# Moving the second batch's first input transfer and its first two transform groups behind the first batch's last transform, in a fused spectral filter and SiLU network

## The chip, the cores and the metric

The kernel runs on one core of one Trainium2 chip. The metric is device time in microseconds (us) of one execution, lower is better. TensorE is called PE below, VectorE DVE, ScalarE ACT, GpSimd POOL and SyncE SP; "SPq" or "ACTq" is such an engine's queue when it issues a DMA transfer.

## The reference, cut to what matters

```python
batch, seq, dim = (8, 3008, 256)
X = np.fft.rfft(x, axis=1)
F = (filt_r + 1j * filt_i)[None, :, :]
y = np.fft.irfft(X * F, n=x.shape[1], axis=1)      # per batch and channel
h = y.reshape(8 * 3008, 256) @ w_in                # w_in: 256 x 2048
g = h * (1.0 / (1.0 + np.exp(-h)))
out = g @ w_out                                    # w_out: 2048 x 256
```

So each of 8 batches is filtered along its sequence of 3008 points, and all 24064 resulting rows go through a two-layer network.

## The kernel before, in words

**The transform.** 3008 is split as 47 x 64 (in fact 94 x 32), and each batch's filter is three stages of small matmuls with tables of cosines and sines. Stage 1 (`stage1`, L339; for the first batch `stage1_first`, L295) takes rows of the input to 94 residues. `forward` (L456), `multiply`, `add` and `inverse` apply the filter. `stage3` (L574) makes the rows of `y`, which the network reads. Between the stages the data changes its layout by a trip through HBM: it is written to a scratch tensor `d1` (after stage 1) or `d2` (after `inverse`) and read back in another order.

**The network.** It is done in 384 steps of 14 matmuls on 128 x 128 tiles (`hidden` and `project`, L743 and L802). In the steady state the next batch's transform is put between these matmuls by a plan of due times (`plan`, L623).

**The ramp.** The first batch has no earlier batch to hide behind. Its whole transform, and the bit-by-bit conversion of the first nine pairs of weight blocks from 64-bit floats (`weights`, `bits`, `converted`, `rounded`, `placed`), run first, in an order written out by hand from L1038 to L1178. The program order of these lines is the order on each engine's queue. What matters for the change:

- `load_two` (L326) loads the second batch's rows for its transform groups 0 and 1: one transfer on SP of 96 rows of 8 KB (768 KB) into `x_all`. Before, it stands at L1113, behind the last `stage1_first`, which read `x_all` for the first batch, and ahead of `weights(8)` (L1114).
- `inverse_first` (L516) and `rows_first` (L531) end the filter for one of six groups `g`. Each group makes two tiles `q` of 256 KB, copied out of PSUM and written to `d2` (L543). ACT copies and issues both tiles of groups 0 to 3 and the first of groups 4 and 5; DVE copies the second tile of groups 4 and 5, and SP issues it. The tiles of group 4 reuse the buffers of group 0, so their copies wait until those transfers have landed.
- `load_t4_rows` (L567) reads the rows back: six transfers of 256 KB on SP (16 rows of 16 KB each), two for each of three parts `k`. Part 2 needs the rows of groups 4 and 5.
- `second["stage1"](u, False)` (L1159) is stage 1 of the second batch for `u` = 0 and 1: two matmuls of 96 x 512 each on PE (L345, four rows of the trace for each `u`) and four copies of the results on ACT (L361). `store_rows` (L369) writes them to `d1` from POOL, four transfers for each `u`; they stand behind a small POOL copy (L1167) that holds POOL until weight block 8 is placed.
- `idle_wide(16)` (L1170) issues 16 matmuls of 96 x 256 whose result nobody reads.
- Four `stage3` groups (L1171) follow, then the reload of the table `wi_t` (L1173), which must wait for them, `load_x(2)` (L1174), which overwrites the buffer that `stage1(0)` reads, and the transfers of later weight blocks.
- Then the network starts with `hidden(0)`, in which L764, L771 and L777 are copies of partial sums on ACT, and L727 combinations on DVE.

Two things are handed out in program order. `bank` (L251) gives each matmul group one of eight PSUM banks in turn, counted by `early[0]`. And in the trace all transfers that SP and ACT issue take eight landing semaphores in turn, in program order; the issue of a transfer waits until the one eight before it has landed.

Of the kernel before, what the change touches and what calls it, by code (L numbers as in the profile page):

```python
# [170 lines left out]
def kernel(  # L171
# [75 lines left out]
    early = [0]  # L247
# [3 lines left out]
    def bank(b, name, spare=None):  # L251


        if early[0] is None and spare in ("x", "yz"):
            return xps.tile([128, 2, C], FP32, name=name, tag=spare)
        if early[0] is None and spare is not None:
            return accps.tile([128, 2, C], FP32, name=name, tag=f"a{spare}")
        if early[0] is None:
            return fps.tile([128, 2, C], FP32, name=name, tag="f")
        early[0] += 1  # L260
        k = early[0] % 8
        if k < 2:
            return fps.tile([128, 2, C], FP32, name=name, tag="f")
        if k > 5:
            return xps.tile([128, 2, C], FP32, name=name, tag="x" if k == 6 else "yz")
        return accps.tile([128, 2, C], FP32, name=name, tag=f"a{k - 2}")
# [688 lines left out]
    def convert_weights(*js):  # L955
        for j in js:
            _, _, e, m, ef, mf, *_ = raws[j]
            nc.scalar.activation(out=ef, in_=e, func=AFT.Relu, bias=bias_t[:, 0:1])
            nc.scalar.activation(out=mf, in_=m, func=AFT.Identity, scale=2.0 ** -20, bias=1.0)
        for j in js:  # L960
            if j in (0, 2, 6, 7, 8):

                e, ef = raws[j][2], raws[j][4]
                nc.scalar.activation(out=ef, in_=ef, func=AFT.Relu, scale=-1.0, bias=bias_t[:, 1:2])
                nc.scalar.activation(out=e, in_=ef, func=AFT.Identity, scale=-float(1 << 23),
                                     bias=bias_t[:, 2:3])
# [42 lines left out]
    def weights(*js, queue=None):  # L1009
        for j in js:  # L1010
            if wide:
                load_weights(j, queue)
# [5 lines left out]
    def converted(*js):  # L1018
        if wide:
            convert_weights(*js)  # L1020
# [9 lines left out]
    def placed(*js, eng=None):  # L1030
        if wide:
            place_weights(*js, eng=eng)
        else:
            for j in js:
                load_exact(j)
# [15 lines left out]
    def idle_wide(n, ps=None, rhs=None):  # L1051

        ps = ps or bank(0, "idle")
        for _ in range(n):
            nc.tensor.matmul(out=ps[:, 0], lhsT=wx_t, rhs=wide_rows if rhs is None else rhs,
                             start=True, stop=True)
# [4 lines left out]
    part, second = spectral(0), spectral(1)  # L1061
# [47 lines left out]
    for k in range(16):  # L1109
        part["stage1_first"](k, 2)  # L1110
        if k in whole:
            part["stage1_first"](whole[k], 3)
    second["load_two"]()  # L1113
    weights(8)  # L1114
    part["forward"](0, fill=4)
    placed(0, 1)
# [34 lines left out]
    for k in range(2):  # L1151
        part["load_t4_rows"](k)
    part["load_t4_rows"](2)
    converted(4, 5)
    placed(2, 3)
    weights(9)
    converted(6, 7)
    for u in range(2):
        second["stage1"](u, False)  # L1159
    converted(8)  # L1160
    rounded(4, 5)
    placed(4, 5)
# [2 lines left out]
    rounded(8)  # L1165
    placed(8)
    gp.tensor_copy(out=gate, in_=w_t[:, 4, A11, 0, 0:1])  # L1167
    for u in range(2):
        second["store_rows"](u)
    idle_wide(16)  # L1170
    for g in range(4):  # L1171
        part["stage3"](g)
    nc.sync.dma_start(out=wi_t, in_=wi_dram.ap())  # L1173
    second["load_x"](2)  # L1174
    weights(10, 11, 12)
# [91 lines left out]
```

## Time and profile before

| | |
|---|---|
| median of 3 runs | 2577.19 us (2576.88 to 2578.64) |
| the profiled execution | 2579.25 us |
| its span in the trace | 2577.4 us |
| PE busy in the span | 2553.1 us, 99% |
| DVE, ACT, POOL busy | 65%, 42%, 17% |
| mean granted PE clock | 0.995 |
| first matmul of `hidden(0)` | 76.94 us |
| DMA in the first 130 us, mean | 223 GB/s |

The views are: the page (busy shares, slices of the span, the chain of work that ended last), the timeline of one engine (start, duration, engine, line, operation, tile written and read, count, and in brackets the idle time before it and what ended it), the windows (busy time by engine, granted PE clock, DMA share and GB/s in a stretch of time), and the chain in order of time (start, duration, what). Rows of the trace for one float32 matmul come in twos: "x32" of `idle` are 16 matmuls.

### The profile page before, as it was taken

Reading aid. Unit: us, or ns where it says so; the run is one execution under the profiler, and the core shown is the slowest. Engines: PE = TensorE matmul, PEld = TensorE weight load, DVE = VectorE, ACT = ScalarE, POOL = GpSimd, SP = SyncE. Lnnn points to the kernel's source line nnn. Section 1 sums busy time; section 2 is a strip of 40 time slices with the busy share of each in tenths; the row PEclk is TensorE's granted clock in tenths of the full one; section 3 lists DMA queues with packets and bytes.
Section 4 is the critical chain, followed back from the end, with each engine's and each line's share of the span. In section 5 each row is a group of like instructions: output and inputs, shape, how many; then the busy total and the mean of one; then the engine's idle time right before and its main releaser. Section 6 shows DMA issues by size and latency. Waiting matters only on the chain.

```text
span 2577.4 us, 47850 instructions
## 1 busy us (share of the span) xinstructions
PE 2553.1 (99%) x18714; PEld 2196.6 (85%) x18714; DVE 1664.4 (65%) x3589; ACT 1090.4 (42%) x3019; POOL 430.3 (17%) x688
## 2 busy tenths in 40 slices
PE   8999999999999999999999999999999999999998
PEld 6688888888888888888888888888888888888987
DVE  7766666676666666666666676666666666555554
ACT  3544444444444444444444444444444444444443
POOL 4212111111122111311121111211121112101101
PEclk9899999999999999999999999999999999999999
DMA  9522232222223222322233122331232211200011
GB/s 291 158 60 52 70 79 63 60 68 72 59 64 69 70 65 55 79 71 67 59 70 80 49 66 59 79 80 46 66 86 64 68 41 34 59 18 16 9 17 16
DMA packets 198554, 171.06 MB, mean 66 GB/s; under 512 B 122068, under 2 KB 173380, under 8 KB 197348
## 3 DMA queue, kind: packets, MB, share of 16 engines
q1 hardware_dynamic: 176056, 117.06, 19.9%
q0 software_dynamic: 17344, 45.70, 5.6%
q10 hardware_dynamic: 4928, 5.24, 0.7%
q8 instruction: 147, 2.41, 0.4%
q14 instruction: 79, 0.65, 0.1%
HBM read 96.07 MB, written 81.26 MB: 69 GB/s over the span
## 4 chain that ended last, share of the span: by engine, by line
PE 96%; DMA 2%; DVE 0%; ACT 0%; issue 0%; SPq 0%; ACTq 0%; DVEq 0%
PE acc L819 44%; PE px L756 26%; PE pyz L756 19%; PE pd L586 3%; PE pb L467 2%; PE pc L510 2%; PE pf L434 1%; DMA filt<-in_filt_i_dram 0%; PE pa L354 0%; DMA w_t<-in_x_dram 0%; DMA d_t<-d_tbl 0%; PE pa L345 0%; DMA x_all<-in_x_dram 0%; DMA d<-q 0%; DMA w_t<-d 0%; DMA t<-d 0%
## 5 line engine op out<-in xcount | busy, mean ns | idle before, releaser
L819 PE MATMUL acc<-g,w_t 128*128 128x256 f32 (+1 forms) x5376 | 1509.2, 375 | 0.4 <-DVE g L727 0.4
L819 PEld LDWEIGHTS acc<-g,w_t 128*128 128x128 f32 x5376 | 1021.6, 190 | 115.7 <-DVE g L727 0.8
L727 DVE TENSOR_TENSOR g<-pyz,abc 128x256 f32<-128x256 f32 (+1 forms) x1152 | 480.0, 417 | 621.6 <-ACT abc L777 356.2
L727 DVE TENSOR_TENSOR g<-g 128x256 f32<-128x256 f32 (+3 forms) x1152 | 599.4, 520 | 196.7 <-ACT g L760 183.5
L756 PE MATMUL px<-ty,w_t 128*128 128x256 f32 (+1 forms) x2304 | 679.4, 377 | 1.1 <-ACT abc L771 0.6
L760 ACT ACTIVATE g<-g 128x256 f32<-128x256 f32 (+1 forms) x1152 | 472.9, 410 | 250.2 <-DVE g L727 250.2
L727 POOL TENSOR_TENSOR s<-s 128x256 f32<-128x256 f32 (+1 forms) x329 | 255.0, 792 | 1417.5 <-DVE s L839 1321.0
L756 PEld LDWEIGHTS px<-ty,w_t 128*128 128x128 f32 x2304 | 432.7, 190 | 65.5 <-issue 6.2
L756 PE MATMUL pyz<-y,w_t 128*128 128x256 f32 (+1 forms) x1536 | 454.0, 377 | 0.0
L756 PEld LDWEIGHTS pyz<-y,w_t 128*128 128x128 f32 x1536 | 283.9, 190 | 47.6 <-DVE g L727 6.8
L771 ACT COPY abc<-px 128x256 f32<-128x256 f32 (+1 forms) x384 | 141.3, 368 | 372.9 <-PE px L756 372.9
L777 ACT COPY abc<-px 128x256 f32<-128x256 f32 (+1 forms) x384 | 141.5, 369 | 339.0 <-PE px L756 338.1
L760 ACT ACTIVATE g<-px 128x256 f32<-128x256 f32 (+1 forms) x384 | 145.8, 380 | 300.9 <-PE px L756 300.8
L756 PE MATMUL px<-y,w_t 128*128 128x256 f32 (+1 forms) x768 | 232.7, 385 | 0.8 <-DVE y L600 0.8
L756 PE MATMUL pyz<-ty,w_t 128*128 128x256 f32 (+1 forms) x768 | 225.8, 376 | 0.3 <-DVE g L727 0.2
L756 PEld LDWEIGHTS px<-y,w_t 128*128 128x128 f32 x768 | 140.4, 190 | 33.0 <-DVE y L606 5.3
L756 PEld LDWEIGHTS pyz<-ty,w_t 128*128 128x128 f32 x768 | 144.5, 190 | 19.2 <-DVE g L727 1.5
L764 ACT COPY abc<-px 128x256 f32<-128x256 f32 (+1 forms) x384 | 135.4, 353 | 52.7 <-PE px L756 52.7
L586 PEld LDWEIGHTS pd<-wi_t,t 48*64 48x64 f32 x3840 | 61.1, 135 | 25.1 <-ACT g L760 16.4
L446 POOL DMA_DIRECT2D d<-tf x144 | 71.6, 504 | 29.2 <-DVE tf L442 29.2
L839 ACT COPY s<-acc 128x512 f32<-128x512 f32 (+1 forms) x94 | 54.2, 577 | 47.6 <-PE acc L819 47.4
L869 DVE STREAM_TRANSPOSE o<-s 128x256 f32<-128x256 f32 x192 | 73.9, 423 | 0.4 <-issue 0.3
(136 smaller groups left out, 1269.9 us busy)
## 6 DMA issues: line engine op xcount, KB each, us to landing
t<-d SPq DMA_DIRECT2D x120, 192.0 KB
t<-d SPq DMA_DIRECT2D x84, 256.0 KB
d<-q POOLq DMA_DIRECT2D x84, 256.0 KB, 2.7
out_dram<-o SPq DMA_DIRECT2D x636, 32.0 KB
d<-tf POOLq DMA_DIRECT2D x144, 96.0 KB, 3.2
xr<-in_x_dram SPq DMA_DIRECT2D x6, 1472.0 KB
x_all<-in_x_dram SPq DMA_DIRECT2D x72, 96.0 KB
x_all<-xr SPq DMA_DIRECT2D x72, 96.0 KB
```

The costliest lines, as they stand in the source:

```text
L446: nc.gpsimd.dma_start(out=d1[k // 2, :, k % 2, n0:n0 + 4], in_=us["tf"][32 * k:32 * k + NS].rearrange("p q n c -> p (q n) c"))
L467: nc.tensor.matmul(out=ps[k][32 * j:32 * j + 32, ri, :], lhsT=d_t[rows, 4 * g + at, ri, :], rhs=rhs, start=True, stop=True)
L586: nc.tensor.matmul(out=ps[h][c0:c0 + 64, cb, i, :], lhsT=t4[rows, i, 128 * cb + c0:128 * cb + c0 + 64], rhs=wi_t[rows, :], start=True, sto ...
L727: eng.tensor_tensor(out=out, in0=in0, in1=in1, op=op)
L756: nc.tensor.matmul(out=out, lhsT=w_t[:, jp, c, 0], rhs=rhs, start=start, stop=True, skip_group_check=True)
L760: nc.scalar.activation(out=g[:, k, 0:n], in_=g[:, k, 0:n] if src is None else src, func=AFT.Silu)
L764: nc.scalar.copy(out=sums[:, 0, 0:n], in_=xo)
L771: nc.scalar.copy(out=sums[:, 1, 0:n], in_=xo)
L777: nc.scalar.copy(out=sums[:, 2, 0:n], in_=xo)
L819: nc.tensor.matmul(out=acc[pair][i][:, h, 0:n], lhsT=w_t[:, jp, c, 1], rhs=g[:, k, 0:n], start=(jp == 0 and h == 0), stop=last, skip_group ...
L839: copy(out=s[:, 2 * i:2 * i + 2, 0:n], in_=acc[pair][i][:, :, 0:n])
L869: v.transpose(out=o[:, :, h, :], in_=results[pair][:, ((2, 6), (4, 1))[chunk][h], :])
```

## The change

`load_two` moves on SP from ahead of `weights(8)` to behind the six read-back transfers. The two `stage1` groups of the second batch move from ahead of `converted(8)` to behind the four `stage3` groups of the first batch. `idle_wide` goes from 16 to 20 and now follows the last `inverse` on PE directly. The bank counter is advanced by 7, so that the groups behind it get other banks.

```diff
             part["stage1_first"](whole[k], 3)
-    second["load_two"]()
     weights(8)
     part["forward"](0, fill=4)
 ...
     part["load_t4_rows"](2)
+    second["load_two"]()
     converted(4, 5)
     placed(2, 3)
     weights(9)
     converted(6, 7)
-    for u in range(2):
-        second["stage1"](u, False)
     converted(8)
 ...
     gp.tensor_copy(out=gate, in_=w_t[:, 4, A11, 0, 0:1])
+    idle_wide(20)
+    early[0] += 7
+    for g in range(4):
+        part["stage3"](g)
+    for u in range(2):
+        second["stage1"](u, False)
     for u in range(2):
         second["store_rows"](u)
-    idle_wide(16)
-    for g in range(4):
-        part["stage3"](g)
     nc.sync.dma_start(out=wi_t, in_=wi_dram.ap())
     second["load_x"](2)
```

## The prediction

> **What bounds the kernel now.** I read the page first: the slices of the granted clock and the chain that ended last.
>
> ```profile
> PEclk9899999999999999999999999999999999999999
> PE 96%; DMA 2%; DVE 0%; ACT 0%; issue 0%; SPq 0%; ACTq 0%; DVEq 0%
> ```
>
> Over 96% of the span PE is the bound. Behind the ramp (to about 87 us) steps of 14 matmuls follow without a gap, at 0.43 us a matmul, and the change takes no matmul out of them. So it is worth what it moves the point where that steady run begins, and nothing else. As that point I take the end of the second matmul of step 1, 86.63 us in the timeline of PE.
>
> Next I read the chain in order of time, for the ramp (start, duration, what).
>
> ```profile
> 43.29 8.54 DMA x_all<-in_x_dram
> ...
> 51.91 0.37 ACTq L543
> ...
> 53.95 3.01 DMA d<-q
> 56.96 0.67 DVE q L541
> ...
> 57.66 4.00 DMA d<-q
> ...
> 62.27 6.70 DMA w_t<-d
> ...
> 69.10 7.12 PE pd L586 x254
> ```
>
> From 43 to 69 us the ramp waits for transfers, and the first of them is `load_two`, which has nothing to do with the first batch. It delays the writes of `d2` twice: they wait behind it in the DMA engines, and the sixth write (51.91) takes its landing semaphore. The trace's landing records give its price. Weight transfers of 256 KB ahead of it land 0.67 us apart (43.69, 44.34, 45.01, 45.71); from 45.71 to 53.69 four more of them and `load_two` land, so `load_two` took 7.98 - 4 x 0.67 = 5.3 us (at least 3.5, the distance from the landing ahead of it, 48.30 to 51.83). Then twelve writes land 0.66 us apart from 54.11 to 61.66: a full queue. The six reads land from 63.20 to 68.97.
>
> Then the timeline of PE:
>
> ```profile
> 53.48 3.70 PE L345 MATMUL pa<-x_all,wx_t 96*128 96x512 f32 x8
> 57.01 7.07 PE L1055 MATMUL idle<-d_t,wx_t 96*128 96x256 f32 x32
> 67.84 0.42 PE L586 MATMUL pd<-wi_t,w_t 48*64 48x47 f32 x2 [3.76 <-DMA w_t<-d]
> 69.10 7.07 PE L586 MATMUL pd<-wi_t,w_t 48*64 48x47 f32 x254 [0.84 <-DMA w_t<-d]
> 76.94 1.19 PE L756 MATMUL px<-y,w_t 128*128 128x256 f32 x2 [0.77 <-DVE y L600]
> ```
>
> The two `stage1` groups (53.48) cost nothing today: PE would wait until 69.1 anyway. Last, windows that I cut at the clock's own steps. It rises at 8.05, falls at 66.07 and rises at 86.55 us, which are 17 and 6 times 3.413 us apart (columns: stretch, then busy us of PE, PE loads, DVE, ACT, POOL; granted clock, DMA share, GB/s).
>
> ```profile
> 62.66:66.07 3.41, 1.42 (x7) 0.92 (x5) 3.34 (x8) 3.38 (x7) 0.00 (x0) 1.00 0.97 231
> 66.07:69.49 3.42, 0.81 (x18) 0.70 (x19) 3.38 (x9) 2.23 (x4) 0.00 (x0) 0.50 0.83 186
> 69.49:72.90 3.41, 3.41 (x140) 3.41 (x136) 2.00 (x5) 0.95 (x3) 0.88 (x3) 0.50 0.03 8
> 72.90:76.31 3.41, 3.28 (x122) 3.11 (x117) 0.61 (x2) 1.31 (x4) 3.37 (x7) 0.50 0.61 156
> 76.31:79.73 3.42, 2.79 (x7) 1.86 (x7) 2.66 (x6) 0.74 (x2) 0.00 (x0) 0.50 0.82 217
> 83.14:86.55 3.41, 3.41 (x8) 2.63 (x9) 2.02 (x6) 1.46 (x4) 0.00 (x0) 0.50 1.08 290
> 11.46:14.87 3.41, 2.37 (x16) 2.18 (x16) 2.64 (x7) 3.38 (x6) 0.00 (x0) 1.00 1.02 432
> ```
>
> A window with PE busy 1.42 of 3.41 us loses the clock, one with 2.37 keeps it. At half clock two windows full of `stage3`'s small matmuls do not bring it back, nor does one with 2.79 us; a full one of large matmuls does (83.14).
>
> **The change, part by part.**
>
> *Landing of the rows.* Without `load_two` ahead, weight 8 lands 5.3 us earlier, the first write at about 48.8 (50.6 by the lower price), and the writes no longer queue: they come as ACT makes them, one each 1.03 us (copies at 44.72, 45.74, 46.77). The tenth on ACT is issued at 45.32 + 9 x 1.03 = 54.6 instead of 56.11. DVE's copy at 54.88 had waited 3.70 us for the buffer of a write that landed at 54.76; now it follows group 4's matmuls at about 51.8 (four `inverse` groups fill 46.38 to 53.48, 1.77 each), then 0.6, four combinations of 1.5 in all, the next copy 0.6: SP issues the last write at about 54.5 instead of 57.66. A 256 KB transfer on a free queue lands 3.0 us after its issue (92.38 to 95.36), two at once 0.66 later: 58.0 instead of 61.66. Semaphores: counted in program order, the sixth write and the reads now wait for weight blocks and early writes that have landed; none waits long. The six reads took 7.3 us behind the last write (61.66 to 68.97): 58.0 + 7.3 = 65.3, a little less since four of them need not wait for the last writes. I take **65.1**, 4.0 earlier. Bounds: 63.7 (the reads at their 1.15 us each from their issue at 55) and 67.
>
> *`idle_wide`.* It starts at 53.48 and lasts 7.07 x 40/32 = 8.8: to 62.3. Idle until 65.1, 2.8 us, against 5.0 before.
>
> *The clock.* In the window that ends at 66.07 PE would be busy 1 us, less than the 1.42 that lost it. So I take it as lost. The trace does not show where between 1.42 and 2.37 the limit lies, how small matmuls count, or whether a run has these window edges.
>
> *`stage3`.* 64 rows take 1.15 us at full clock (at 156.26), 256 take 4.6; at half clock 7.1. From 65.1 to 66.07, 21% is done; the rest takes 5.6: 71.7.
>
> *`stage1`, now on the path.* 1.72 us each at full clock (89.22 to 90.94), 6.9 for both at half. It is dense enough to bring the clock back after one full window: at 76.31 on these edges, with 4.6 of 6.9 done, and the rest takes 1.15: 77.5 (over all edges 76.9 to 78.6). This is where most of the 4.0 us goes.
>
> *`hidden(0)`.* Before, 76.94 to 84.99, all at half clock. At full clock its first combination on DVE comes 1.1 us after the start instead of 2.16; from there DVE's queue (weight 9, 4.14 us to the combination at 83.24) is the same; then one matmul: 6.2 us instead of 8.05. Tokens and `y` copies, which held it for 0.77 us, now lie beside `stage1`. Step 1 starts at 83.7, two matmuls end at 84.6, against 86.63: **-2.0**.
>
> *At nothing, with its cover.* `load_two` lands 3.5 to 5.3 us behind the last read, 68.6 to 70.4; PE asks at 71.7. If late, its delay is paid in full. Weight 9 goes behind it, at about 72; DVE first reads it some 2.5 us into `hidden(0)`. `stage1`'s ACT copies (2.03 us) leave the conversion of weights, which DVE follows, and go beside PE; the last ends some 0.6 us after `stage1`, before `hidden(0)`'s first copy is due. `load_x(2)` and the weights behind it on SP now wait for `stage1(0)`, not only for `stage3`: about 75 instead of 76.6; weight 10 landed at 81.61 and is read at 88.47. POOL's eight stores move behind these copies, to about 76 to 80; nobody reads `d1` before step 10. The eight banks of the moved groups were evicted before 57 us, or stand behind work of PE itself.
>
> Sum: -2.0 here, -1.9 over all window edges. On the profiled execution 2579.25 - 1.9 = 2577.3; the median of the runs lies 2.06 lower, so **2575.3**.
>
> [...]
>
> **Rivals.**
>
> *The clock is kept.* For it: the gap shrinks from 5.0 to 2.8 us, and 2.37 of 3.41 us was enough. Against: `stage3` behind it did not count as full at half clock. Then 65.1 + 4.6 + 3.45 + 6.2 + 0.86 = 80.2, so -6.4: 2570.8.
>
> *The clock is lost a second time.* `hidden(0)` at full clock has 7 x 0.43 = 3.0 us of matmuls in 6.2: 49%, between the two known windows. One more stretch at half clock costs 2 to 3 us: 2577.8.
>
> *Slower: the rows do not come earlier.* If the reads are bound by themselves (16 KB rows, 1.15 us a transfer at 180 to 250 GB/s) or by what I miss on DVE, they land at 69 as before; `stage1` then has no cover. `stage3` to 76.2, `stage1` with the clock back at 79.73 to 81.4, `hidden(0)` to 87.6, 88.5 against 86.63: +1.9, 2579.1. It decides from a landing later than about 67. Against it: the twelve landings 0.66 apart and DVE's 3.70 us wait.
>
> *`load_two` does not leave the path*: it holds PE in `stage1` or slows the reads. About 2577.
>
> **How the numbers follow.** Forecast 0.55 (2573.2 to 2576.5); clock kept 0.15; lost again 0.15; rows not earlier 0.1; `load_two` in the way 0.05. The range takes in the kept clock and the late rows with 0.4 on top: 2570.3 to 2579.5. A measurement here can tell 0.2%, 5.2 us: faster than that is nearly only the kept clock, 0.16; slower needs late rows and a second loss, 0.05; the rest 0.79.
>
> **What would show it.** Right: no `load_two` between the writes; the last write landing near 58; `stage3` at 65 on PE; half clock until about 76; `hidden(0)` at 77 to 78 and as long as 6.2 us. Wrong: an idle PE ahead of `stage1`, rows at 67 or later, full clock through `stage3`, or gaps in steps 1 to 6.

## The result and the profile after

| | before | after |
|---|---|---|
| median of 22 runs each | 2577.46 us | 2581.02 us |
| lowest to highest | 2575.38 to 2581.01 | 2579.50 to 2582.91 |
| ratio, 95% interval | | 1.0014 [1.0007, 1.0020] |
| profiled execution / its span | 2579.25 / 2577.4 us | 2582.52 / 2580.7 us |

The changed kernel is 3.6 us slower. Forecast was 1.9 us faster. Both profiled executions lie above their medians, by about as much (1.8 and 1.5 us).

On the page almost nothing moves: PE is still the bound for 96% of the chain.

```profile
PEclk9899999999999999999999999999999999999999
PE 96%; DMA 2%; DVE 1%; ACT 1%; issue 0%; ACTq 0%; SPq 0%; DVEq 0%
```

The chain in order of time, changed kernel, around the change (start, duration, what; a DMA piece runs from its issue to its landing):

```profile
54.81 0.59 ACT q L541
55.43 5.18 DMA d<-q
60.74 0.48 SPq L571
61.27 6.93 DMA w_t<-d
68.33 7.07 PE pd L586 x254
75.40 6.65 PE pa L345 x8
82.05 0.43 PE px L756 x2
```

`x_all<-in_x_dram` has left the chain, as meant, and the last write of `d2` is issued at 55.43 instead of 57.66. But that write now takes 5.18 us to land instead of 4.00, the last read lands at 68.20 (61.27 + 6.93) instead of 68.97, and a new piece stands behind `stage3`: 6.65 us of `pa`, the moved `stage1`.

The timeline of PE of the changed kernel:

```profile
54.18 8.90 PE L1055 MATMUL idle<-d_t,wx_t 96*128 96x256 f32 x40
67.37 0.28 PE L586 MATMUL pd<-wi_t,w_t 48*64 48x47 f32 x2 [4.29 <-issue]
68.33 7.07 PE L586 MATMUL pd<-wi_t,w_t 48*64 48x47 f32 x254 [0.68 <-DMA w_t<-d]
75.33 6.72 PE L345 MATMUL pa<-x_all,wx_t 96*128 96x512 f32 x8
81.89 0.60 PE L756 MATMUL px<-y,w_t 128*128 128x256 f32 x2
```

The pause ahead of `stage3` is 5 us (63.08 to 68.33, with 0.28 us of work in it), as long as before. `stage1` takes 6.72 us where the same matmuls took 3.70 in the kernel before: the clock is at half. The windows show why (columns as in the prediction):

```profile
64.36:67.77 3.41, 0.28 (x2) 0.19 (x2) 3.38 (x8) 1.40 (x3) 0.00 (x0) 1.00 0.96 223
...
78.01:81.43 3.42, 3.42 (x5) 1.35 (x4) 0.00 (x0) 1.18 (x3) 1.40 (x3) 0.50 0.37 86
```

PE works 0.28 of the 3.41 us that end at 67.77, and the clock falls there. It comes back at 81.43, behind the first window filled by `stage1` alone; nearly all of `stage1` ran at half clock.

**How to compare two executions.** The code up to the last `inverse` matmul has the same instructions on PE in both kernels, and yet that matmul ends at 53.55 in the one trace and 54.25 in the other; over the traces below it is 51.2 to 53.3, once 56.6. Times below with a plus sign are therefore counted from the end of that matmul. So counted, the second matmul of step 1 comes 1.7 us later in the changed kernel. Of the 3.3 us between the two profiled executions 0.7 lie ahead of the change, 1.7 in it and 0.9 behind, in the steady run. The steady run differs by as much between kernels that share it (from the 101st row of the output matmuls to the last: 2425.2 to 2427.0 us, run 8 left aside), so I do not put the 0.9 down to the change.

### The profile page after: what moved, and what is told of

The parts are those of the page before. It is cut to its first block, busy times and chain, and to the rows that moved or that the text cites. A ratio compares the mean times of both kernels' runs of the same rounds, so it can differ in the third digit from the quotient of the medians.

```text
span 2580.7 us, 47871 instructions
## 1 busy us (share of the span) xinstructions
PE 2554.5 (99%) x18722; PEld 2197.6 (85%) x18722; DVE 1664.0 (64%) x3589; ACT 1091.9 (42%) x3019; POOL 430.9 (17%) x688
## 4 chain that ended last, share of the span: by engine, by line
PE 96%; DMA 2%; DVE 1%; ACT 1%; issue 0%; ACTq 0%; SPq 0%; DVEq 0%
PE acc L819 44%; PE px L756 26%; PE pyz L756 19%; PE pd L586 3%; PE pb L467 2%; PE pc L510 2%; PE pf L434 1%; DMA filt<-in_filt_r_dram 1%; PE pa L345 1%; PE pa L354 0%; DMA w_t<-in_x_dram 0%; DMA e_t<-e_tbl 0%; DMA w_t<-d 0%; DVE g L727 0%; ACT q L541 0%
```

## The experiments

Each was timed over five rounds against the kernel before on the same chip. Single traces shift by up to 2 us, so verdicts on time rest on the medians and the traces tell where the time is.

**1. Only `stage1` late.** The changed kernel, with `load_two` back at its old place.

```diff
+    second["load_two"]()
     weights(8)
 ...
-    second["load_two"]()
     converted(4, 5)
```

> This is the changed kernel with load_two back in its old place; only stage1 of the second batch (and the longer idle_wide in front) is moved. Theory (moving stage1 onto PE's path costs more than load_two's move gives): the writes and reads of d2 stand as in the kernel before, the rows land about 69.0 to 69.7 us, stage3 runs at half clock to about 76.5, stage1 takes 6.7 at half clock; the time is 1 to 1.5 us above the changed kernel: about 2582.3, and about 5 above the kernel before. Rival (load_two's new place gives nothing at all, everything comes from stage1): equal to the changed kernel, 2581.0. Rival (load_two's new place itself costs time): below the changed kernel, 2579 or less.

Measured: 2582.92 us, ratio 1.0021 [1.0012, 1.0030]. So by the medians the late `stage1`, with the longer `idle_wide`, costs 5.4 us, and the late `load_two` gives back 1.9. The two halves of the change have opposite signs. The intervals of this run and of the whole change overlap, so the 1.9 is not sure by time alone; the traces have the same sign (with `load_two` late the rows land 0.95 us earlier and step 1 is reached 1.0 earlier). The late `load_two` alone cannot be had: `stage1` reads what it brings. In this run's timeline of PE the `stage1` on the path is the same:

```profile
67.27 7.07 PE L586 MATMUL pd<-wi_t,w_t 48*64 48x47 f32 x254 [0.43 <-DMA w_t<-d]
74.27 6.76 PE L345 MATMUL pa<-x_all,wx_t 96*128 96x512 f32 x8
```

The trace accounts for 2.7 of the 5.4 us: `stage1` with the half clock 5.76 more between `stage3` and `hidden(0)`, rows 0.53 earlier, `hidden(0)` at full clock 2.54 less (up to step 1). This execution was the fastest of its eleven; what the others had more, no trace shows.

**2 and 3. Other target partitions, every third.** `SPREAD` in the changed kernel and in the kernel before.

```diff
-SPREAD = (32, 1), (1, 2), (0, 2)
+SPREAD = (0, 3), (1, 3), (2, 3)
```

> The changed kernel, with the 48 rows of each half read back to every third partition (SPREAD (0,3), (1,3), (2,3)) instead of (32,1), (1,2), (0,2); the table ws follows. In the changed kernel the two transfers of the part that goes to 16 neighbouring partitions have 16 KB packets of about 2.06 us each, those of the spread parts 1.1 us. Theory (the reads are bound by where they go: neighbouring partitions are slower): all six go at 1.1 us or less, the last lands about 2 us earlier, near 66 instead of 68.2, and the time falls by about 2 us to 2579. Rival (the reads are bound by where they come from, 16 KB rows of the scratch tensor): packets and landing stay, 2581.0.

> The kernel before with the rows read back to every third partition, nothing else changed. Theory (neighbouring target partitions bind the reads of part 0; in the kernel before these two transfers took 3.3 us, beside the last writes, instead of 2.2): rows about 1 us earlier, 2576.2. Rival (bound by where they come from): 2577.2 as before.

Measured: 2583.22, ratio 1.0021 [1.0012, 1.0029], and 2579.29, ratio 1.0004 [0.9996, 1.0013]. No gain, so this expectation of mine failed as to time. The packets show why. Each read is moved in 16 packets, one row of 16 KB each. In the kernels as given the first two reads go to 16 neighbouring partitions, the other four to every second one. In the changed kernel the packets of the second read take about 2.07 us, those of the last three 1.11; the first (0.8 to 1.4) and the third (1.3 to 2.0) overlap with what stands beside them. In the kernel before the second and third have 1.5 to 1.6, the last three 1.07. With every third partition most packets take 1.2 to 1.6 us. The packet times of all six reads, added up and divided by the 16 DMA engines, are 8.1 us in the changed kernel and 7.7 in run 2, 7.0 in the kernel before and 8.6 in run 3. Which partitions a transfer fills does set its time, but this spread mostly evens it out. In the kernel before with this spread the rows landed at +16.95 instead of +15.42. Run 3's times lie apart: eight of eleven from 2579.15 to 2579.80 us, three from 2574.50 to 2576.29.

**4. Enough idle matmuls to bridge the pause in the changed kernel.** `idle_wide(32)` for `idle_wide(20)`.

> The changed kernel with idle_wide(32) instead of 20: PE's filler ends about 68, when the rows land, so that no idle window takes the clock ahead of stage3. Theory A (the clock is lost by the idle gap alone): stage3 4.6 us instead of 7.07 and stage1 3.45 instead of 6.65, so 5.7 us less: about 2575.3. Theory B (stage3's small matmuls lose the clock themselves within a window): stage3 5 to 6, stage1 partly at half clock: 2578 to 2579.5. If the granted clock has no part in it: 2581.0.

Measured: 2580.64, ratio 1.0013 [1.0004, 1.0022]. 220 of the 256 rows of `stage3` in the trace took 3.64 us, at full clock, and yet `stage3` was little shorter: 6.8 us up to `stage1`, against 7.0 in the changed kernel. Its timeline of PE:

```profile
67.38 3.64 PE L586 MATMUL pd<-wi_t,w_t 48*64 48x47 f32 x220
73.44 0.78 PE L586 MATMUL pd<-wi_t,w_t 48*64 48x47 f32 x36 [2.43 <-issue]
74.16 7.09 PE L345 MATMUL pa<-x_all,wx_t 96*128 96x512 f32 x8
```

After 220 matmul rows PE stops for 2.43 us, for nothing that the profile shows as a wait. As the stop begins, a 16 KB transfer of the instruction queue starts (70.87 us, 1.1 us long). Runs 5, 9, 10 and 11 have such a stop too. In all five it stands ahead of the 285th matmul row behind the last `inverse`, however many of these rows are idle matmuls, and it ends 1.4 to 1.6 us after the end of such a transfer. In the other traces PE comes to this row 1.2 us or more after the end of that transfer, and the step there is at most 0.31 us. So the stop belongs to one place in PE's instructions and to that transfer. That PE waits there for its own instructions is my reading of this; no wait in the profile shows it. The stop leaves 0.98 us of work in the window that ends at 74.20, the clock falls, and `stage1` is at half clock again.

**5. The same in the kernel before.** `idle_wide(27)` for `idle_wide(16)`.

> The kernel before with idle_wide(27) instead of 16: the filler then ends near 69, when the rows land, and PE has no gap ahead of stage3. In the run of the changed kernel with a longer filler, stage3 kept the full clock (220 rows in 3.64 us) until PE stopped for 2.43 us with nothing in the profile to wait for, beside a 16 KB transfer of the instruction queue. Theory (the half clock in stage3 and hidden(0) is worth its price here too): stage3 4.4 instead of 7.1, with a stop of up to 2.4, hidden(0) 6.3 to 8 us: 2573 to 2577. Rival (the stop for instructions and a second loss of the clock eat the gain, as they did there): 2577.5 or above.

Measured: 2577.55, ratio 0.9998 [0.9989, 1.0007]. `stage3` at full clock (220 rows in 3.47 us, then a stop of 0.92), but the clock falls in `hidden(0)`, at 79.83, behind this window:

```profile
76.41:79.82 3.41, 1.75 (x6) 0.89 (x6) 3.34 (x10) 2.19 (x5) 0.00 (x0) 1.00 0.88 279
```

`hidden(0)` has pauses for ACT (1.17 and 0.46 us) and DVE (0.15 and 0.16), and PE is busy 1.75 of 3.41 us. This is the second loss that the prediction had as a rival. The median shows no gain.

**6 and 7. The second read of each part (partitions 64 and up) on POOL's queue.** In the kernel before and in the changed one; the lines are cut at the right.

```diff
-                (queue or nc.sync).dma_start( ...
+                (queue or (nc.sync, nc.gpsimd)[h]).dma_start( ...
```

> The kernel before, but the rows of the upper half of the partitions (64 and up) are read back by POOL instead of SP, so that a transfer to the lower and one to the upper half can run side by side. Theory (each read is bound by the few partitions it goes to, not by the scratch tensor, the 16 DMA engines or the landing of the writes): the six reads take 4 to 5 us instead of 7.3 behind the last write, rows near 66 instead of 69, time 3 us less: 2574.5. Rival (bound by source, engines or the last write): rows near 69, 2577.5; POOL's slower issue may even cost 1.

> The changed kernel with the same reads on two queues. Theory: the writes are issued by 55.4 and landed by 60.6 there, and the reads no longer take 7.6 us behind them but 4: rows near 64.5 instead of 68.3, the gap ahead of stage3 shrinks to about 1.5 us, time 3.5 to 5 less: 2576 to 2577.5, about as the kernel before, since stage1 stays on the path. Rival (bound by source, engines or the last write): 2581.

Measured: 2576.58, ratio 0.9996 [0.9987, 1.0005], and 2581.81, ratio 1.0017 [1.0008, 1.0026]. Neither differs from the kernel it was made from, so the gain that I expected came in neither. The packets of the last three reads take 1.03 to 1.09 us each and follow one another, whichever queue they come from; here a second queue adds no second stream. POOL's issue was no slower: 0.48 to 0.59 us each in both runs, where SP took 0.36 to 0.59 in the kernel before. The rows land at +15.24 and +14.20, against +15.42 and +13.94.

**8. `stage1` out of the ramp altogether.** The changed kernel with the two groups put into the plan of the network's steps 1 to 8, and their lines in the ramp removed, with those of `load_x(2)` and `load_x(3)`, which the plan then holds.

```diff
-            for u in range(2, 8):
-                put(at + u - 49, 3, part["stage1"], u)
+            for u in range(8):
+                put(at + u - 47, 3, part["stage1"], u)
 ...
-    for u in range(2):
-        second["stage1"](u, False)
-    for u in range(2):
-        second["store_rows"](u)
 ...
```

> The changed kernel, but stage1 of the second batch for u = 0 and 1 is not behind stage3: all eight groups go into the plan of the steady run, one in each of steps 1 to 8, and the weight blocks 10 to 13 are loaded without load_x between. Theory (the loss of the change is stage1's 6.6 us at half clock): stage1 costs 3.4 at full clock there, hidden(0) starts about 76 at half clock and takes 8.0 instead of 6.3; 6.6 - 3.4 - 1.8 = 1.4 less than the changed kernel: 2579.6, still above the kernel before, in which these matmuls cost nothing. Rival (the loss lies elsewhere, in transfers or ACT): no better than 2581.

Measured: 2581.74, ratio 1.0017 [1.0008, 1.0026]. Without `stage1` the ramp ends earlier than before: the second matmul of step 1 ends at +31.2, against +33.1. But the two groups then cost 2 x 1.72 us inside full steps, and the median is where the changed kernel's is, 2.1 us above my expectation; about 1 us more in the trace's steady run is not explained. Of the two other places tried for `stage1`, behind `stage3` and in the plan, neither is free; the wait for the rows was.

**9. Every fourth partition, in the kernel before.** The 48 rows of a half are spread over 64 partitions; `stage3` contracts over 64, the 16 between them with zero weights.

```diff
-SPREAD = (32, 1), (1, 2), (0, 2)
+SPREAD = (0, 4), (1, 4), (2, 4)
 ...
-    ws_host = wi_host.copy()
+    ws_host = 0 * wi_host
 ...
-  rows = slice(64 * h, 64 * h + 2 * NS)
+  rows = slice(64 * h, 64 * h + (64 if b == 0 and g < 4 else 2 * NS))
```

> The kernel before, with its six reads put on every fourth partition of a half (first partition 0, 1 and 2), and the ramp's stage3 contracting over 64 partitions instead of 48, the 16 between with zero weights. Theory (the partitions that a transfer writes set how long its 16 KB packets take: 16 neighbours 2.06 us, every third 1.5 us, every second 1.07 us): all six packets take about 1.07 us, so the six reads need 6.5 us instead of 8.5 us, the rows land about 2 us sooner after the end of the last inverse (13.4 us instead of 15.4 us), and stage3 begins there: about 2575.5 us, ratio 0.999. Rival (the sum of the six packets is a fixed cost that only shifts from one packet to another, as it did with every third partition: 6 times 1.45 us is 8.7 us): packets near 1.4 us each, rows at 15.4 us, 2577.4 us. A second rival for the time alone: packets are shorter, but the clock's fall gives the gain back by the next stage, within 0.5 us of the kernel before.

Measured: 2573.91, ratio 0.9987 [0.9978, 0.9996]: 3.3 us faster than the kernel before, and the fastest of all. The chain of this kernel:

```profile
55.85 3.96 DMA d<-q
59.89 0.47 SPq L571
60.40 5.79 DMA w_t<-d
66.33 3.78 PE pd L586 x242
70.11 1.26 issue
71.38 0.48 PE pd L586 x12
```

The rows land at +13.25 instead of +15.42, as expected to 0.2 us. The six reads land within 6.4 us of the last write, not 7.3; the writes themselves landed 1.25 us earlier, which this edit does not touch and which I count as scatter. So of the 2.2 us the reads give 0.9; their packets take 6.0 us an engine, not 7.0. The pause ahead of `stage3` is short enough here that the clock stays: 3.78 us for 242 rows. It falls only in `hidden(0)`, at 78.45. The kept clock, on which the expectation had not counted, goes with a median 1.6 us below it. The edit changes the target partitions and the contraction together, and no run has one without the other.

**10. The same with `idle_wide(22)`.**

> As the run with every fourth partition, and idle_wide(22) instead of 16 ahead of the kernel before's stage3. Theory: the rows land about 2 us sooner, the idle matmuls end about 2 us later than the 16 did, so the pause before stage3 falls from 5 us to under 2 us, and stage3 runs at full clock (about 3.6 us for its 220 matmuls behind the first groups, not 6.6 us). If the clock then holds through hidden(0): 2577.4 - 2 - 3 = about 2572.5 us. Rival, from the run with idle_wide(27) in the kernel before: the clock is lost again in hidden(0) and nothing of the second gain is left: about 2575.5 us, as without the idle matmuls.

Measured: 2575.49, ratio 0.9994 [0.9986, 1.0003]; not better than run 9. The profiled execution had landed its rows at 67.96, with PE still in the idle matmuls, to 69.74. But it is 3.0 us slower than the median and not typical: its clock fell once more at 48.04, ahead of the edit, and its last `inverse` ended at 56.61, 3.7 us later than in run 9. Counted from there the idle matmuls end at +13.13, about where the rows of run 9 land (+13.25). The clock is lost again in `hidden(0)`, at 82.17, as the rival had it; what else costs the median 1.6 us against run 9 stays open.

**11. Every fourth partition, in the changed kernel.**

> The changed kernel with its six reads on every fourth partition. Theory: its rows land about 2 us sooner too (12 us after the end of the last inverse instead of 14 us), stage3 follows, stage1 stays behind it on the path at half clock: 2581.3 - 2 = about 2579.3 us, still about 2 to 4 us over the kernel before with the same reads. Rival (the reads are a fixed sum): 2581.3 us.

Measured: 2577.11, ratio 1.0000 [0.9991, 1.0009]: 3.9 us better than the changed kernel, and 3.2 us behind run 9. The rows land at +12.06 instead of +13.94, 5.43 us after the issue of the last read and not 6.93, though the last write landed only 0.3 us earlier than there (+6.04). From its chain:

```profile
53.70 4.43 DMA d<-q
...
58.72 5.43 DMA w_t<-d
```

The timeline of PE shows `stage1` at full clock for once, and still on the path:

```profile
64.29 6.24 PE L586 MATMUL pd<-wi_t,w_t 64*64 64x47 f32 x242 [0.39 <-DMA w_t<-d]
...
71.15 3.70 PE L345 MATMUL pa<-x_all,wx_t 96*128 96x512 f32 x8
```

Counted to the first matmul of `hidden(0)`, against run 9: rows 1.2 us earlier, `stage3` 1.5 longer (half clock), then 3.47 us to `hidden(0)` instead of 0.77. Together +3.0 of trace, 3.2 by the medians.

**12. Run 11 with `idle_wide(25)`**, to take the half clock out of `stage3` as well.

> The changed kernel with its six reads on every fourth partition and idle_wide(25) instead of 20. Question: is stage1's price on the path its own 3.5 us of PE, or only the half clock. Idle matmuls end about 1.1 us later, the window before stage3 then holds about 2.5 us of PE work; windows of the earlier runs with 1.91 us or more kept the clock. Theory (stage1's own time): stage3 runs in 3.7 us at full clock plus a stop of 0.3 to 1.3 us, stage1 in 3.5 us, about 2 us less than without the added idle matmuls: 2575 to 2576 us, which is still 1 to 2 us over the kernel before with the same reads (2573.9 us), since 3.5 us of stage1 are on the path and only 1.2 us of earlier rows and 0.8 us of the wait for y stand against it. Rival (only the half clock made stage1 dear): 2573.9 us or less.

Measured: 2577.16, ratio 1.0005 [0.9996, 1.0014]; no gain, and the question it was to settle is not settled cleanly, since the clock fell all the same. Its eleven times spread from 2575.84 to 2582.31 us, six up to 2577.16 and five from 2579.37, and the trace is of one of the six. Two windows, of run 12 (the clock falls at its end) and of run 10 (it stays):

```profile
62.33:65.74 3.41, 1.81 (x32) 1.26 (x31) 3.38 (x8) 2.00 (x4) 0.00 (x0) 1.00 0.89 209
```

```profile
71.92:75.34 3.42, 1.91 (x117) 1.66 (x108) 0.77 (x2) 1.47 (x4) 3.08 (x7) 1.00 0.38 91
```

What run 12 does show is `stage1` once more at full clock, 3.5 us from the end of `stage3` to `hidden(0)`: the least that it cost there in any trace.

## Why the prediction was wrong

The failed step is *Landing of the rows*: "The six reads took 7.3 us behind the last write ... I take **65.1**, 4.0 earlier." They landed at 68.20, 67.5 if the 0.7 us ahead of the change are taken off. What happened is the rival that had 0.1, "the rows do not come earlier", as to its mechanism: the reads are bound by themselves. By its own terms that rival gave +1.9 us at step 1; the traces give +1.7. That these agree is partly luck: the rival had the rows 1.5 us later than they came and `stage1` 1.4 us shorter than it was.

| step | predicted | measured in the changed kernel |
|---|---|---|
| last write issued | 3.15 us earlier | 2.9 earlier (+1.17 against +4.11) |
| last write landed | 3.7 earlier | 1.75 earlier (+6.36 against +8.12) |
| rows landed | 3.9 earlier | 1.5 earlier (+13.94 against +15.42) |
| pause ahead of `stage3` | 2.8 us | 5 us |
| `stage3` | 6.6 us | 7.07 us |
| `stage1` | 5.8 us | 6.56 us to `hidden(0)` |
| `hidden(0)`, to its last matmul | 6.2 us | 6.28 us |
| `load_two` landed, needed | 68.6 to 70.4, 71.7 | 71.51, 75.33 |
| second matmul of step 1 | -2.0 | +1.7 |

The removal worked up to the issue. Weight block 8 and the writes no longer queue behind `load_two`, ACT issues a write each 1.03 us, DVE's wait of 3.70 us is gone. From there two sizes were wrong. Along the prediction's own chain 1.9 of the 2.4 us are missed at the last write, 0.3 behind it (7.59 us for "7.3") and 0.2 in taking 65.1 for 65.3. But an earlier last write would hardly have helped. The packets of the six reads follow one another from 58.2 to 59.0 us on until 66.3 to 67.4, and the two reads that wait for the last writes were issued at 60.74 and 61.27, with earlier reads still running.

*The last write.* I took 3.0 us from issue to landing, from a transfer in the steady run. The last two writes have 14 of their 16 parts in HBM by 58.1 and 59.1 us; the last part lands at 60.08 and 60.61. A 16 KB transfer of the instruction queue ran from 56.63 for 1.62 us, and the packets that trail go on as it ends. In run 8 the same is seen (15 parts by 57.5, the last at 59.0; the transfer ended at 57.3). That this transfer and those packets share one DMA engine is my reading of these times and not shown: the trace does not number the engines, and I did not try to move that transfer.

*The reads.* I carried over "7.3 us behind the last write" as if it were a latency. It is a duration: in both kernels the six reads follow each other, first parts landing 2.1 us apart after the first read and 1.1 to 1.2 apart from then on (changed kernel: 60.61, 62.70, 63.86, 64.98, 66.09, 67.21). In the kernel before, the first of them ran beside the last writes, so the distance from the last write was shorter than their sum. With the writes out of the way they still need 8.1 us of packets an engine. I had the hint in the text ("16 KB rows, 1.15 us a transfer") and gave it 0.1, against the evenly spaced writes; those spoke of the writes only (and were 0.69 us apart on average, not 0.66).

Runs 2, 3, 9 and 11 show what binds them: the partitions they fill. Six transfers to every third partition bring the rows no earlier, six to every fourth do, in both kernels (packets 7.0 to 6.0 us an engine in the kernel before, 8.1 to 5.7 in the changed one). A 16 KB packet took 2.07 us with 16 neighbouring partitions (the second read of the changed kernel; in the kernel before, beside the last writes, 1.5 to 1.6), 1.0 to 1.1 with every second one (the last three reads), 1.5 with every third (run 3, nearly all 16 packets of a read), and by the sums above 1.0 or a little less with every fourth. Why neighbours are slow, and why every third partition is slower than every second, no run shows, nor what sets the 1.07 us that are left.

*The clock.* Taken as lost, and lost; the terms grew because the fall came ahead of all of `stage3`, and the first window full of `stage1` ended 6.1 us after its start instead of 4.6. My gap of 2.8 us never came about. Where the limit lies, left open in the prediction between 1.42 and 2.37 us of work in a window, the runs bring together: lost behind 0.98, 1.45, 1.60, 1.65, 1.75, 1.79 (run 11) and 1.81 us, kept behind 1.87 (2569.75 to 2573.16 in the changed kernel), 1.91, 2.02, 2.10 and more, with one exception in run 10, lost behind 1.99:

```profile
44.62:48.04 3.42, 1.99 (x35) 1.02 (x35) 3.42 (x7) 2.63 (x7) 3.42 (x6) 1.00 1.05 265
```

So by these runs the limit is near 1.9 us, and busy time as the profile counts it does not give it exactly. In the window of run 12 the longest gap was 0.95 us and the clock fell. In run 9 a window with a gap of 1.32 us and 2.10 us of work (61.38 to 64.80) kept it. In these runs the share of work in the window tells the outcome better than the longest gap.

*`stage1`.* The prediction knew that it would be uncovered and that most of the gain would go there. It was mis-sized by 0.8 us. What it did not draw from this: the move pays for a sure 3.5 us or more on PE's path with a hoped-for transfer gain, and by the terms measured here the rows would have had to come 3.2 us earlier to break even (1.5 + 1.7). They came 1.5 earlier.

*The sum.* The four terms off by +2.4 (rows), +0.5, +0.8 and +0.1 (rounded) turn -2.0 into +1.7 at step 1, what the traces have. The medians are apart by 3.6, with an interval of 1.8 to 5.2; the rest is not located. Part of it may lie in the one trace of the kernel before. Compared with it from the last `inverse` to the end, each of the other thirteen traces comes out better than by the medians, by 0.2 to 3.6 us, so that trace seems to be a slow one in this part.

## What to carry to other kernels

Work that lies under a wait is free only there. Before moving it to shorten the wait, ask how long the thing waited for takes by itself, with nothing ahead of it: that is the least that the wait can shrink to, and it must shrink by more than the moved work. A transfer's duration behind another is not its own duration (here the six reads landed 7.3 us behind the last write in the kernel before, and took 8.1 us of packets an engine in the changed one); and where a read-back bounds, look first at which partitions its rows fill, since here that edit, with the contraction that it needs, brought 3.3 us with nothing moved.

## What the runs showed of the hardware that I had not expected

- Beside a 16 KB transfer of the instruction queue (56.63 us, 1.62 us long) the last parts of the last two writes trailed: they landed 2.0 and 1.5 us behind the 14th of 16, at 60.08 and 60.61, and the read that waited for the later one was issued at 60.74. That the transfer holds one of the 16 DMA engines is my estimate from these times.
- In `stage3` at full clock PE stopped after 220 to 242 rows for 0.92 to 2.43 us, with no wait in the profile (runs 4, 5, 9 and 10), always ahead of the 285th matmul row behind the last `inverse`. At half clock there was no such stop, or one of 0.26 us (run 11).
- Two queues for the six reads did not overlap their 16 KB packets: those of the last three still took 1.03 to 1.09 us each, one behind another (runs 6 and 7).
- To bring the clock back, a window with 3.41 us of the 48-row matmuls of `stage3` was not enough, nor a second one behind it (3.28 us in the kernel before, 3.41 in run 3); in runs 11 and 12, with 64 rows, one window was (3.42 and 3.41 us). A window filled by `stage1` (3.42 us) brought it back in the changed kernel; in run 4 the first one did not, and the second did:

```profile
74.20:77.62 3.42, 3.42 (x5) 1.46 (x5) 2.09 (x4) 1.06 (x2) 0.00 (x0) 0.50 0.07 12
77.62:81.03 3.41, 3.41 (x5) 1.35 (x4) 0.00 (x0) 1.17 (x2) 2.12 (x4) 0.50 0.52 129
```

  Busy time alone does not tell these apart, and what the chip counts is not shown.
